# V in 1024-byte rows with its history copied on chip, head loads in other pieces, and a new written order

## The chip, the core and the metric

One core of a Trainium2 chip runs the whole program. It has a matrix engine (TensorE, PE in the profile; its weight loads are PEld), VectorE (DVE), ScalarE (ACT), GpSimd (POOL) and SyncE (SP), which here only issues DMA. Each engine works through its own list of instructions in order and waits on semaphores for the others. The metric is the device time of one launch in microseconds; the runs shown are compared by their median.

## What is computed

A block with adaptive layer norm: an attention over a dilated local window, then a gated FFN. S = 2048 rows, D = 512, 32 heads of 16, window of 8 keys at distance 2, FFN width 1792, all bf16.

```python
mod = (_silu(c) @ w_mod).reshape(c.shape[0], 6, 1, -1)
sa, ca, ga, sb, cb, gb = (mod[:, 0].copy(), ..., mod[:, 5].copy())
h = _layernorm(x, axis=-1) * (1 + ca) + sa
x = x + ga * _A_ref(h, A_wqkv, A_wo)
h = _layernorm(x, axis=-1) * (1 + cb) + sb
x = x + gb * _B_ref(h, B_w_gate, B_w_up, B_w_down)
...
# _A_ref: q, k, v from x @ wqkv; each query sees the keys at pos - 2*w, w = 0..7
logits = jnp.einsum('bhsd,bhswd->bhsw', q, kg) * scale
logits = jnp.where(mask[None, None, :, :], logits, -1000000000.0)
attn = _softmax(logits, axis=-1)
o = jnp.einsum('bhsw,bhswd->bhsd', attn, vg)
...
# _B_ref
h = _gelu(g) * u
return jnp.einsum('bsf,fd->bsd', h, w_down)
```

## The kernel before

The 2048 rows run as four groups (sg 0 to 3) of 512. For each group:

- `norm`, `norm_act`, `rst`, `norm_x`: statistics of x on DVE (`bn_stats`, `bn_aggr`, the "pair"), for some row blocks on ACT; a power on POOL gives 1/std; DVE writes the normalised `xn`, one instruction for each of four row blocks.
- xn is turned into hT (columns on partitions) and scaled by the modulation. There are three ways: for group 0 by PE transposes (`transp0`) with evictions on DVE and ACT (`transp0_ev`); for group 1's first norm and group 0's second (`BY_PE`) by PE transposes with evictions on ACT; for all others by a DMA transpose from SP (`transp`, L490), after which POOL (group 2's first norm, `H_POOL`) or ACT multiplies in place (`transp_ev`, L525 and L527).
- `qkv`: twelve blocks of four 512-column matmuls, the query, key and value rows with heads spread over partitions; ACT evicts them (`qkv_ev`). For group 0 the first two query blocks are made in halves of 256 columns (`qkv_halves`).
- `logits`: four DVE products `pq` of q with eight shifted views of kT (4096 elements per partition each), summed over the head's elements by PE matmuls with 32 output rows (`logits_mm`, the tile LTp). `soft`: max, subtraction, sum, reciprocal and product on DVE, the exponential on ACT; its result is `e`.
- `e` is spread to `PT`, for group 0 by PE and ACT (L736, L745), for the others through DRAM (`pt_dma`).
- V goes through DRAM: `vload` stores `vT` to `vscr` and reads it back four times (w4 = 0 to 3) into 32 partitions each of `V4`, each shifted by two rows more. Group sg reads 512 + 8 columns, the 8 being history from the group before; the zeros ahead of group 0 are written by POOL memsets.
- `pv`: four DVE products of PT and V4, summed by PE matmuls with 32 output rows (`pv_mm`, o_ps); `pv_ev` evicts to oT on ACT; `x1_mm` multiplies by wo, whose tile `woP` DVE has scaled by the gate `gB` (`woscale`); `x1_ev` adds to x.
- `ffn_mm`: 14 pairs of g and u (four matmuls each), gelu and eviction on ACT, product `hht` on DVE, then y by 56 matmuls and the addition `ot` on DVE, and the store.

The gates reach `gB` through DRAM (`gload`: a store of 1 KB and a broadcast read). Twenty warm-up matmuls (`warmup`) keep PE busy from the start until data is there; the first 11 run ahead of the transposition of silu(c).

Every step is an `Op` in one of 135 generators ("threads"), with an engine and the names it must come after. The list `ORDER` names, for the whole program, which thread gives its next step; this fixes the order on every engine, including the order in which SP issues its DMAs. Hardware DMAs share eight completion semaphores in rotation, so a DMA also waits until the one eight places ahead of it has landed.

SP's DMAs go out in this order at first: x of group 0 (half), the modulation columns 1 and 0 (`ldwm01`), wqkv0, x1, wqkv1, x2, wqkv2, the modulation columns 2 and 3, x3, four wo.

Of the kernel before, what the change touches and what calls it, by code (L numbers as in the profile page):

```python
# [106 lines left out]
def kernel(  # L107
# [23 lines left out]
    VH = 16  # L131
    VR = S + VH

# [5 lines left out]
    NB = {"x": 4, "hT": 2, "xn": 2, "q": 4, "vs": 1, "v4": 1, "prod": 5, "h2": 2,  # L139
# [17 lines left out]
    maskT = const.tile([H, W, 16], F32, name="maskT")  # L157
# [12 lines left out]
    kT = const.tile([P, 4, 3 * SG + 16], BF16, name="kT")  # L170

# [9 lines left out]
    def setup():  # L181
# [27 lines left out]
        yield Op("POOL", 3.0, f2, take=[SL["v4"]], fire="M2", after=["LN1.0.rs2"])  # L209
# [11 lines left out]
    def loads():  # L221
# [51 lines left out]
        def act_q():  # L273
            yield Op("ACT", 0.46, ldx(0, 2, 4, nc.scalar), fire="x0.2", lat=mb(0.25), dma=True)
            yield Op("ACT", 0.45, ldc, fire="c", lat=0.0, dma=True)
        qs = [act_q()]
        def head_q():
            yield Op("SP", 0.47, ldx(0, 0, 2), fire="x0.0", lat=mb(0.25))
            for b in (1, 0):
                yield Op("SP", 0.5, lambda b=b: ldwm01(b), take=[SL["prod"]] if b else [], fire=f"wm{b}", lat=mb(0.5))  # L280
# [697 lines left out]
```

## Time and profile before

| | us |
|---|---|
| median of 3 runs | 236.9 |
| lowest, highest | 236.7, 237.16 |
| span of the profiled execution | 234.1 |

How to read the profile: it shows one execution. Busy time is given per engine; matmuls are pipelined, so a single one's duration (379 ns for 512 columns) is longer than the distance from one to the next. The chain of waits goes back from the last instruction: at each step to what released it, or to the instruction ahead of it on its engine. A row of a timeline has start, duration, engine, source line, operation, output <- inputs, shapes, the number of instructions merged in it, and in brackets how long the engine stood idle before it and what ended that. "SPq" rows are DMA issues. In the tables by window the pairs are busy us and number of instructions for PE, PEld, DVE, ACT and POOL, then the granted clock, the DMA engines' share and GB/s.

The program reads 22.37 MB from HBM and writes 4.98 MB; SP's DMA queue keeps 16 DMA engines busy for 50.6% of the span, with 36265 packets in all, 14872 of them under 512 bytes.

### The profile page before, as it was taken

What the parts mean: (1) busy time and instruction counts of PE and PEld (TensorE: products, weight loads), DVE (VectorE), ACT (ScalarE), POOL (GpSimd) and SP (SyncE); (2) the same over time, 40 slices, a digit from 0 to 9 for tenths busy, and PEclk for the clock granted to TensorE, in tenths of its full rate; (3) what the DMA queues carried; (4) which work ended last, traced back from release to release, by engine and by line L of the source; (5) the groups of instructions that cost most, each with busy time, mean ns of one, the idle gap of its engine ahead of it and who ended that gap; (6) DMA issues with size and microseconds to landing.
All of it is one profiled execution on the core that took longest, in us unless ns stands there. A gap on an engine that the chain in (4) does not pass through costs nothing.

```text
span 234.1 us, 3675 instructions
## 1 busy us (share of the span) xinstructions
PE 230.0 (98%) x1387; PEld 108.2 (46%) x1387; DVE 170.4 (73%) x240; ACT 150.0 (64%) x283; POOL 18.6 (8%) x43
## 2 busy tenths in 40 slices
PE   7999999999999999999999999999999999999995
PEld 2755455434644444444444444444444444444443
DVE  3999999999997999999799788467747421222222
ACT  4899997976997758936656492546754343666400
POOL 2612461000100000100000010000001000000000
PEclk9999999999999999999999999999999999999999
DMA  6997989999969839553102963510000411000011
GB/s 218 373 364 213 202 213 171 276 391 303 176 152 236 291 92 200 98 114 103 56 0 57 202 109 60 156 56 0 0 4 0 90 45 45 3 0 0 0 48 45
DMA packets 36265, 30.21 MB, mean 129 GB/s; under 512 B 14872, under 2 KB 34328, under 8 KB 36248
## 3 DMA queue, kind: packets, MB, share of 16 engines
q1 hardware_dynamic: 35968, 29.72, 50.6%
q10 hardware_dynamic: 280, 0.26, 0.3%
q8 instruction: 11, 0.18, 0.3%
q14 instruction: 6, 0.05, 0.1%
HBM read 22.37 MB, written 4.98 MB: 117 GB/s over the span
## 4 chain that ended last, share of the span: by engine, by line
PE 98%; DVE 0%; issue 0%
PE g_ps L844 21%; PE u_ps L844 21%; PE y_ps L856 19%; PE qkv_ps L598 17%; PE x_ps L811 6%; PE o_ps L790 3%; PE LTp L678 3%; PE warm_ps L217 3%; PE y_ps L868 1%; PE qkv_ps L580 1%; PE hTp L484 1%; PE hTp L509 0%; PE modT_ps L305 0%; PE modT_ps L348 0%; PE gR_ps L369 0%; PE PTp L736 0%
## 5 line engine op out<-in xcount | busy, mean ns | idle before, releaser
L844 PE MATMUL g_ps<-h,Wg 128*128 128x512 bf16 x224 | 57.5, 379 | 0.0
L844 PE MATMUL u_ps<-h,Wu 128*128 128x512 bf16 x224 | 57.5, 379 | 0.0
L878 ACT ACTIVATE gl<-g_ps 128x512 bf16<-128x512 f32 x56 | 33.6, 600 | 24.8 <-PE g_ps L844 23.9
L856 PE MATMUL y_ps<-Wd,hht 128*128 128x512 bf16 x210 | 46.0, 379 | 0.0
L885 ACT CAST ub<-u_ps 128x512 bf16<-128x512 f32 x56 | 32.8, 586 | 18.3 <-PE u_ps L844 18.1
L598 PE MATMUL qkv_ps<-hT,wqkv 128*128 128x512 bf16 x184 | 42.1, 380 | 0.0
L896 DVE TENSOR_TENSOR hht<-gl,ub 128x512 bf16<-128x512 bf16 x56 | 23.0, 421 | 25.3 <-ACT ub L885 25.0
L664 DVE TENSOR_TENSOR pq<-qT,kT 128x4096 bf16<-128x4096 bf16 x16 | 36.3, 2292 | 0.0
L771 DVE TENSOR_TENSOR pv<-PT,V 128x4096 bf16<-128x4096 bf16 x16 | 36.0, 2286 | 0.0
L844 PEld LDWEIGHTS <-Wg 128*128 128x128 bf16 x224 | 21.5, 98 | 27.3 <-issue 2.1
L844 PEld LDWEIGHTS <-Wu 128*128 128x128 bf16 x224 | 21.8, 98 | 26.6 <-issue 0.4
L856 PEld LDWEIGHTS <-hht 128*128 128x128 bf16 x210 | 20.5, 98 | 24.8
L598 PEld LDWEIGHTS <-wqkv 128*128 128x128 bf16 x184 | 20.1, 114 | 19.7 <-issue 3.0
L903 DVE TENSOR_TENSOR ot<-y_ps,x 128x512 bf16<-128x512 f32 x15 | 10.3, 689 | 20.2 <-PE y_ps L856 17.2
L471 POOL TENSOR_TENSOR rstd<-rstd,neghalf 128x4 f32<-128x4 f32 (+1 forms) x9 | 8.8, 980 | 154.1 <-DVE rstd L460 85.5
L527 ACT ACTIVATE h<-h,modT,scl 128x512 bf16<-128x512 bf16 x12 | 8.8, 802 | 11.6 <-DMA h<-xn 11.6
L811 PE MATMUL x_ps<-woP,oT 128*128 128x512 bf16 x64 | 15.3, 379 | 0.0
L430 DVE BATCH_NORM_STATS2 st<-x 128x6 f32<-128x512 bf16 x19 | 12.9, 680 | 3.1 <-DMA x<-in_A_x_dram 2.9
L820 DVE TENSOR_TENSOR x<-x_ps,x 128x512 bf16<-128x512 f32 x16 | 10.8, 686 | 5.0 <-PE x_ps L811 5.0
L801 ACT CAST oT<-o_ps 128x512 bf16<-128x512 f32 x16 | 8.9, 592 | 2.7 <-PE o_ps L790 2.7
L618 ACT CAST qT<-qkv_ps 128x512 bf16<-128x512 f32 x16 | 9.2, 587 | 2.2 <-PE qkv_ps L598 2.1
L620 ACT CAST kT<-qkv_ps 128x512 bf16<-128x512 f32 x16 | 9.5, 596 | 1.2 <-PE qkv_ps L598 1.2
(85 smaller groups left out, 181.5 us busy)
## 6 DMA issues: line engine op xcount, KB each, us to landing
V<-vscr SPq DMA_DIRECT2D x12, 520.0 KB, 10.4
wm<-in_w_mod_dram SPq DMA_DIRECT2D x6, 512.0 KB, 5.4
vscr<-vT SPq DMA_DIRECT2D x4, 512.0 KB, 4.2
out_dram<-ot SPq DMA_DIRECT2D x15, 128.0 KB, 1.7
Wg<-in_B_w_gate_dram SPq DMA_DIRECT2D x1, 1792.0 KB, 11.0
Wu<-in_B_w_up_dram SPq DMA_DIRECT2D x1, 1792.0 KB
wqkv<-in_A_wqkv_dram SPq DMA_DIRECT2D x3, 512.0 KB, 8.3
x<-in_A_x_dram SPq DMA_DIRECT2D x3, 512.0 KB, 8.6
```

The lines of the kernel that those rows point to most:

```text
L430: nc.vector.bn_stats(out=st[:], in_=src()[:, c4, :])
L598: nc.tensor.matmul(ps[:], lhsT=wqkv[blk][:, dt, j::4], rhs=B["hT", sg][:, :, dt, :], start=(dt == 0), stop=(dt == DT - 1))
L664: nc.vector.tensor_tensor(out=pq[:], in0=_ap(B["qT", sg][:, j, :], [[0, W], [1, SG]]), in1=_ap(kT[:, j, sg % 3 * SG + 2:sg % 3 * SG + 2 + ...
L771: nc.vector.tensor_tensor(out=t[:], in0=_ap(B["PT", sg][:, 0, :], [[SG, 2], [0, 4], [1, SG]]), in1=_ap(v[:, 0, j, :], [[8, 2], [4 * (SG + ...
L811: nc.tensor.matmul(ps[:], lhsT=B["oT", sg][:, j, c4::CPS] if sg else B["oT", sg][:, j, c4 * P:(c4 + 1) * P], rhs=woP[:, j, :], start=(j == ...
L820: nc.vector.tensor_tensor(out=x[:, c4, :], in0=B["x1ps", sg, c4][:], in1=x[:, c4, :], op=ALU.add)
L844: nc.tensor.matmul(ps[:], lhsT=Wt[:, dt, ft * P:(ft + 1) * P], rhs=B["h2T", sg][:, :, dt, :], start=(dt == 0), stop=(dt == DT - 1))
L856: nc.tensor.matmul(ps[:], lhsT=B["hh", sg, ft][:, c4 * P:(c4 + 1) * P], rhs=B["Wd", ft // 4][:, ft % 4, :], start=(ft == 0), stop=(ft == F ...
L878: nc.scalar.activation(out=gl[:], in_=B["g", sg, ft][:], func=ACT.Gelu_apprx_tanh)
L885: nc.scalar.copy(out=ub[:], in_=B["u", sg, ft][:])
L896: nc.vector.tensor_tensor(out=hh[:], in0=B["gl", sg, ft][:], in1=B["ub", sg, ft][:], op=ALU.mult)
L903: nc.vector.tensor_tensor(out=ot[:], in0=B["y", sg, c4][:], in1=B["x", sg][:, c4, :], op=ALU.add)
```

## The change

- V: rows in `vscr` start at 64 elements instead of 16, each read is exactly 512 elements (1024 bytes) into columns 16 on of one fixed tile `V4`; the eight columns of history are copied within `V4` by POOL (`vhist`) once the group before has used them; the zeros ahead of group 0 come from one POOL memset and from 16 zero columns stored to `vscr` (`vzero`). The reads are a thread of their own (`vread`).
- Head: the modulation columns 0 and 1 are loaded as four pieces of 128 rows x 1024 columns (2048-byte rows) instead of two column blocks, and PE adds up their product piece by piece; wqkv0 is loaded in two halves; c is loaded from GpSimd's DMA queue instead of ACT's.
- Group 0: PE transposes one row block at a time; DVE and ACT share the evictions in another split (`ONV` for `PART`); three query blocks instead of two are made in halves; two warm-ups fewer. The mask tile becomes bf16.
- `ORDER` is another list. On SP, x1 now goes out ahead of the modulation pieces; wqkv0's halves, x2, wqkv1, wqkv2, modulation 2 and 3, the zero columns, x3 and modulation 4 follow. Among other moves: two `bn_stats` pairs of x1 stand on DVE ahead of group 0's last xn and its hT; group 2's first xn stand on DVE behind all four pq of group 0, and group 3's behind group 0's e and the second pq of group 1; the store of the first gate and the read of gB stand on SP behind group 3's DMA transpose, modulation 5 and two wo; three of V's four reads for group 1 stand behind the store of group 1's e; for group 1's second norm the first `ot` stands on DVE ahead of the four xn; in group 2 a pv stands between its second and third xn; group 3's second norm feeds g after 42 of group 2's y matmuls, the rest of which comes later.

```diff
-    VH = 16
+    VH = 64
     VR = S + VH
+    VW = SG + 16
...
-    maskT = const.tile([H, W, 16], F32, name="maskT")
+    maskT = const.tile([H, W, 16], BF16, name="maskT")
...
+    V4 = const.tile([P, 4, 4, VW], BF16, name="V4")
...
-            B["V4", 0] = T("v4", [P, 4, 4, SG + 8], BF16, "V4")
-            for w4 in range(4):
-                nc.gpsimd.memset(B["V4", 0][H * w4:H * w4 + H, :, :, 0:8 + 2 * w4].rearrange("p i j s -> p (i j) s"), 0.0)
+            nc.gpsimd.memset(V4[:, :, :, 0:16].rearrange("p i j s -> p (i j) s"), 0.0)
...
-        def ldwm01(b):
-            if "wm01" not in B:
-                B["wm01"] = T("prod", [P, 2, 4, D], BF16, "wm01")
-            nc.sync.dma_start(out=B["wm01"][:, b, :, :], in_=w_mod[:, b * D:(b + 1) * D].rearrange("(t p) n -> p t n", p=P))
+        def ldwm01(kt):
+            if kt == 0:
+                B["wm01"] = T("prod", [P, 4, 2 * D], BF16, "wm01")
+            nc.sync.dma_start(out=B["wm01"][:, kt, :], in_=w_mod[kt * P:(kt + 1) * P, 0:2 * D])
 
         def ldc():
-            nc.scalar.dma_start(out=c4[:], in_=c.rearrange("o (t p) -> (o t) p", p=P))
+            nc.gpsimd.dma_start(out=c4[:], in_=c.rearrange("o (t p) -> (o t) p", p=P))
...
+            for a in range(2):
+                yield Op("SP", 0.5, ld(wqkv[0][:, 2 * a:2 * a + 2, :], wq_v[:, 2 * a:2 * a + 2, 0:D]), fire=f"wqkv0.{a}", lat=mb(0.25))
...
+                for ch in range(8):
+                    nc.tensor.matmul(B["mp01"][:, ch:ch + 1], lhsT=B["wm01"][:, kt, ch * P:(ch + 1) * P],
+                                     rhs=scT[:, kt:kt + 1], start=(kt == 0 and ch == 0), stop=(kt == 3 and ch == 7))
...
-    PART = ((0, (0, 1), False), (0, (2, 3), True), (1, (0,), False), (1, (1, 2, 3), True))
+    ONV = {(0, True): (0, 2), (0, False): (1, 3), (1, True): (0, 1, 2), (1, False): (3,)}
...
+        for dt in range(DT):
+            def f(dt=dt):
+                for j in range(3):
+                    if dt == 0:
+                        B["qkvps", 0, 0, j] = T("mm", [P, SG], F32, "qkv_ps")
+                    mm(0, j, dt, dt)
...
+        for j in range(3):
+            def f(j=j):
+                for dt in range(DT):
+                    mm(1, j, dt, dt)
...
+    def vzero():
+        yield Op("SP", 0.6, lambda: nc.sync.dma_start(out=vscr[:, :, VH - 16:VH], in_=kT[:, :, 0:16]), after=["M2"],
+                 fire="vz", lat=1.2)
+
     def vload(sg):
         def f():
             nc.sync.dma_start(out=vscr[:, :, VH + sg * SG:VH + (sg + 1) * SG], in_=B["vT", sg][:])
...
+    def vhist(sg):
+        if sg:
+            def f():
+                nc.gpsimd.tensor_copy(out=V4[:, :, :, 8:16].rearrange("p i j s -> p (i j) s"),
+                                      in_=V4[:, :, :, VW - 8:VW].rearrange("p i j s -> p (i j) s"))
+            yield Op("POOL", 0.5, f, after=[f"pv.{sg - 1}.3"], fire=f"vh.{sg}")
+
+    def vread(sg):
         for w4 in range(4):
             def f(w4=w4):
-                if w4 == 0 and sg:
-                    B["V4", sg] = T("v4", [P, 4, 4, SG + 8], BF16, "V4")
-                z = 0 if sg else 8 + 2 * w4
-                src = bass.AP(vscr.tensor, vscr.offset + VH + sg * SG - 8 - 2 * w4 + z,
-                              [[16 * VR, H], [VR, 16], [1, SG + 8 - z]])
...
+                src = bass.AP(vscr.tensor, vscr.offset + VH + sg * SG - 2 * w4, [[16 * VR, H], [VR, 16], [1, SG]])
+                nc.sync.dma_start(out=V4[H * w4:H * w4 + H, :, :, 16:VW].rearrange("p i j s -> p (i j) s"), in_=src)
...
-                                        in1=_ap(v[:, 0, j, :], [[8, 2], [4 * (SG + 8), 4], [1, SG]]), op=ALU.mult)
...
+                                        in1=_ap(V4[:, 0, j, 8:16], [[8, 2], [4 * VW, 4], [1, SG]]), op=ALU.mult)
...
-    pl.spawn(warmup(13, 20))
+    pl.spawn(warmup(13, 18))
```

More of the change, by code (lines that the diff above doesn't have):

```diff
@@ L205, in f2 @@
                                         base=-H * w4, channel_multiplier=1)
[L206 to L209 removed]
+            nc.gpsimd.memset(V4[:, :, :, 0:16].rearrange("p i j s -> p (i j) s"), 0.0)
+        yield Op("POOL", 2.2, f2, fire="M2", after=["LN1.0.rs2"])
     def warmup(cold, n):
@@ L274, in act_q, with pool_q @@
             yield Op("ACT", 0.46, ldx(0, 2, 4, nc.scalar), fire="x0.2", lat=mb(0.25), dma=True)
-            yield Op("ACT", 0.45, ldc, fire="c", lat=0.0, dma=True)
-        qs = [act_q()]
+        def pool_q():
+            yield Op("POOL", 1.0, ldc, fire="c", lat=0.3, dma=True)
+        qs = [act_q(), pool_q()]
         def head_q():
             yield Op("SP", 0.47, ldx(0, 0, 2), fire="x0.0", lat=mb(0.25))
-            for b in (1, 0):
-                yield Op("SP", 0.5, lambda b=b: ldwm01(b), take=[SL["prod"]] if b else [], fire=f"wm{b}", lat=mb(0.5))
+            for kt in range(4):
+                yield Op("SP", 0.5, lambda kt=kt: ldwm01(kt), take=[] if kt else [SL["prod"]], fire=f"wm01.{kt}", lat=0.635)
+            for a in range(2):
+                yield Op("SP", 0.5, ld(wqkv[0][:, 2 * a:2 * a + 2, :], wq_v[:, 2 * a:2 * a + 2, 0:D]), fire=f"wqkv0.{a}", lat=mb(0.25))
         qs.append(head_q())
-        for b in range(3):
+        for b in range(1, 3):
             qs.append(one("SP", 0.55, ldq(b), fire=f"wqkv{b}", lat=mb(0.5)))
@@ L545, in f @@
                         nc.scalar.activation(out=o, in_=i, func=ACT.Identity, scale=sc(dt), bias=bi(dt))
-                yield Op("DVE" if onv else "ACT", 0.32 if onv else 0.455, f, after=[f"{ev}.th{half}"] + dep,
-                         take=[SL["hT"]] if dt == 0 and half == 0 else [], give=[SL["mm" if half else "att"]] if n == len(dts) - 1 else [],
-                         fire=f"{ev}.h{dt}.{half}")
+                give = [] if dt != ONV[half, eng][-1] else [SL["att"]] if half == 0 else [SL["lg" if eng else "mm"]]
+                yield Op("DVE" if eng else "ACT", 0.32 if eng else 0.455, f, after=[f"{ev}.th{2 * half + 1}"] + dep,
+                         take=[SL["hT"]] if dt == 0 and half == 0 else [], give=give, fire=f"{ev}.h{dt}.{half}")
     stat = pool("stat_p", 4)
@@ L570, with mm @@
     QKV = [(0, 0), (1, 0), (2, 0), (2, 1), (2, 2), (2, 3), (0, 1), (1, 1), (0, 2), (1, 2), (0, 3), (1, 3)]
-    QKV0 = [(0, 0), (0, 1), (0, 2), (1, 0), (1, 1), (0, 3), (1, 2), (2, 0), (2, 1), (2, 2), (2, 3), (1, 3)]
+    QKV0 = [(0, 0), (0, 1), (0, 2), (0, 3), (1, 0), (1, 1), (1, 2), (2, 0), (2, 1), (2, 2), (2, 3), (1, 3)]
     def qkv_halves():
-        for half in range(2):
-            for n, dt in enumerate(((2, 0, 3, 1), (0, 1, 2, 3))[half]):
-                def f(half=half, n=n, dt=dt):
-                    for j in range(2):
-                        if half == 0 and n == 0:
-                            B["qkvps", 0, 0, j] = T("mm", [P, SG], F32, "qkv_ps")
-                        nc.tensor.matmul(B["qkvps", 0, 0, j][:, half * 256:half * 256 + 256],
-                                         lhsT=wqkv[0][:, dt, j::4], rhs=B["hT", 0][:, 2 * half:2 * half + 2, dt, :],
-                                         start=(n == 0), stop=(n == DT - 1))
-                yield Op("PE", 0.218, f, after=[f"LN1.0.h{dt}.{half}", "wqkv0"],
-                         take=[SL["mm"]] * 2 + [SL["q"]] if half == 0 and n == 0 else [], fire=f"qph.{half}.{dt}")
-        for j in range(2):
-            pl.done[f"qp.0.0.{j}"] = pl.done["qph.1.3"]
+        def mm(half, j, dt, n):
+            nc.tensor.matmul(B["qkvps", 0, 0, j][:, half * 256:half * 256 + 256], lhsT=wqkv[0][:, dt, j::4],
+                             rhs=B["hT", 0][:, 2 * half:2 * half + 2, dt, :], start=(n == 0), stop=(n == DT - 1))
+        for dt in range(DT):
[4 more added lines that the diff above has]
+                    mm(0, j, dt, dt)
+            yield Op("PE", 0.328, f, after=[f"LN1.0.h{dt}.0", f"wqkv0.{dt // 2}"],
+                     take=[SL["mm"]] * 3 + [SL["q"]] if dt == 0 else [], fire=f"qph.{dt}")
+        for j in range(3):
+            def f(j=j):
+                for dt in range(DT):
+                    mm(1, j, dt, dt)
+            yield Op("PE", 0.437, f, after=[f"LN1.0.h{dt}.1" for dt in range(DT)], fire=f"qp.0.0.{j}")
     def qkv(sg):
@@ L591, in qkv @@
         for n, (blk, j) in enumerate(QKV if sg else QKV0):
[L592 removed]
+            if (sg, blk) == (0, 0) and j < 3:
                 continue
@@ L601, in qkv @@
             tk = {0: [SL["q"]], 1: [], 2: [SL["vs"]]}[blk] if j == 0 else []
-            yield Op("PE", 0.856, f, after=[f"LN1.{sg}.h{d}" for d in (("0.1", "1.0", "3.1") if sg == 0 else (2, 3))] + [f"wqkv{blk}"], take=[SL["mm"]] + tk,
+            yield Op("PE", 0.856, f, after=[f"LN1.{sg}.h{d}" for d in (("2.1", "3.1") if sg == 0 else (2, 3))] + ([f"wqkv{blk}"] if blk else []), take=[SL["mm"]] + tk,
                      give=[SL["hT"]] if last else [], fire=f"qp.{sg}.{blk}.{j}")
@@ L769, in f @@
                 B["pv", sg, j] = t
-                v = B["V4", sg]
                 nc.vector.tensor_tensor(out=t[:], in0=_ap(B["PT", sg][:, 0, :], [[SG, 2], [0, 4], [1, SG]]),
-                                        in1=_ap(v[:, 0, j, :], [[8, 2], [4 * (SG + 8), 4], [1, SG]]), op=ALU.mult)
-            yield Op("DVE", 2.2, f, after=[f"pt.{sg}.1", f"V4ld.{sg}"], take=[SL["prod"]] * heads(GV[sg]).get(j, 0),
-                     give=[SL["v4"], SL["PT"]] if j == 3 else [], fire=f"pv.{sg}.{j}")
+                                        in1=_ap(V4[:, 0, j, 8:16], [[8, 2], [4 * VW, 4], [1, SG]]), op=ALU.mult)
+            yield Op("DVE", 2.2, f, after=[f"pt.{sg}.1"] + [f"V4.{sg}.{w}" for w in range(3)] + [f"V4ld.{sg}"]
+                     + ([f"vh.{sg}"] if sg else ["M2"]), take=[SL["prod"]] * heads(GV[sg]).get(j, 0),
+                     give=[SL["PT"]] if j == 3 else [], fire=f"pv.{sg}.{j}")
     def pv_mm(sg):
```

73 lines of the change are left out of this document (34 added, 39 removed), and 70 rows, old and new, of the table ORDER.

## The prediction

> **What bounds it now.** The page first: the span, the busy shares, and the shares of the chain that ended last.
>
> ```profile
> span 234.1 us, 3675 instructions
> PE 230.0 (98%) x1387; PEld 108.2 (46%) x1387; DVE 170.4 (73%) x240; ACT 150.0 (64%) x283; POOL 18.6 (8%) x43
> ...
> PE 98%; DVE 0%; issue 0%
> ```
>
> TensorE (PE) is never without work: the chain is one row of matmuls. Nothing that only makes DMA lighter can pay. Three things can move the end: the time before the first useful matmul, the sum of the matmuls, and gaps that the new order opens. The chain in order of time (start, duration, what) gives the first two, and I read it next.
>
> ```profile
> 1.25 4.88 PE warm_ps L217 x11
> ...
> 10.07 1.85 PE qkv_ps L580 x16
> 11.93 7.77 PE qkv_ps L598 x36
> 19.70 0.45 PE hTp L484 x8
> ...
> 21.79 0.49 PE modT_ps L305 x16
> 22.28 0.55 PE LTp L678 x8
> ...
> 29.56 10.48 PE qkv_ps L598 x48
> ...
> 80.00 0.22 PE gR_ps L369 x16
> 80.23 0.43 PE o_ps L790 x8
> 80.66 0.97 PE g_ps L844 x4
> 81.63 0.86 PE u_ps L844 x4
> ...
> 97.64 12.09 PE y_ps L856 x56
> ```
>
> Useful work starts at 10.07. Four matmuls of 512 columns cost 0.86. Eight matmuls with 32-row outputs cost 0.43 inside a group of such, 0.55 as the first of one, and the four 512-column ones after the group 0.97 in place of 0.86: each group of 32-row work costs 0.12 + 0.11 = 0.23 of switching.
>
> **The sum of the matmuls.** After the head, PE's built order has 15 such groups before and 10 after: the matmuls of logits, of o and of the gates' rows are gathered. The counts are equal, but for eight more of 256 columns and four fewer of 512, which is even. Gain: 5 x 0.23 = **1.15 us**, all ahead of group 1's FFN (the 2048 rows run as groups 0 to 3).
>
> **The head.** Timeline of DVE and ACT (start, duration, what, idle before in brackets):
>
> ```profile
> 4.12 0.69 DVE L430 BATCH_NORM_STATS2 st<-x 128x6 f32<-128x512 bf16 x1 [2.94 <-DMA x<-in_A_x_dram]
> 4.60 0.31 ACT L328 ACTIVATE s<-c 4x128 bf16<-4x128 bf16 x1 [1.32 <-DMA c<-in_c_dram]
> 4.95 0.66 DVE L430 BATCH_NORM_STATS2 st<-x 128x6 f32<-128x512 bf16 x1
> 8.01 0.41 DVE L448 TENSOR_SCALAR xn<-x,mv,rstd 128x512 bf16<-128x512 bf16 x1 [0.27 <-POOL rstd L471]
> 8.34 0.41 DVE L448 TENSOR_SCALAR xn<-x,sums,rstd 128x512 bf16<-128x512 bf16 x1
> 8.98 1.68 DVE L543 TENSOR_SCALAR hT<-hTp,mod 128x256 bf16<-128x256 bf16 x5
> ```
>
> DVE works from 4.12 to 10.66 with hardly a pause but 0.27 us, so it, not the modulation rows, sets when hT is there. The new order puts two statistics pairs of x1 ahead of hT, 0.83 each (4.12 to 4.95). They fill the pause; and mod now stands before the last xn, which covers part of its latency, as the pairs cover that of the small operations: I take 0.4 for it, of the 8.98 - 8.34 - 0.41 = 0.23 seen there and as much again. So the last hT is done at 10.66 + 1.66 - 0.27 - 0.4 = 11.65 and the first (0.40 long, of five in 1.68) at 10.4; bounds 10.0 and 10.8. The 24 quarter matmuls at 1.85/16 = 0.116 end at 10.4 + 2.8 = 13.2, with three query blocks done; before, three were done at 11.93 + 0.86 = 12.8. Loss **0.4**. The two dropped warm-ups pay nothing, as PE waits for hT in their place.
>
> The head's loads, by windows (last column GB/s) and the tile view of wqkv:
>
> ```profile
> 5.00:10.00 5.00, 5.00 (x62) 2.98 (x61) 4.52 (x17) 4.09 (x11) 3.19 (x11) 1.00 1.07 365
> ...
> L223 SPq DMA_DIRECT2D wqkv<-in_A_wqkv_dram x3: 437/510/563, 2.4 to 5.0; - x3
> ...
> DMA to landing us min/median/max: 6.6/8.3/9.6
> ```
>
> wqkv0 stood behind 1.5 MB and landed at 2.4 + 6.6 = 9.0. After, x1's 0.5 MB goes ahead of the modulation rows, so their last piece takes that place, 9.0, and wqkv0's halves land 0.26 MB / 0.365 = 0.7 later each, at 9.7 and 10.4. The piece is wanted by 9.2 for a mod at 9.55, the halves at 10.4 and 11.1: covered, but by 0.2 at the tightest; what it is late beyond that the head loses. c landed at about 4.5 on ACT's queue. On GpSimd's it has no row; landing anywhere from 3 to 6 it moves only warm-ups, so no cost (rival C).
>
> **V.** PE waited for none of these:
>
> ```profile
> V<-vscr SPq DMA_DIRECT2D x12, 520.0 KB, 10.4
> vscr<-vT SPq DMA_DIRECT2D x4, 512.0 KB, 4.2
> ...
> PT<-escr SPq DMA_DIRECT2D x12, 64.0 KB, 2.4
> ...
> gB<-gscr SPq DMA_DIRECT2D x2, 128.0 KB, 2.8
> ```
>
> Lighter reads are therefore worth 0. The history copy waits on POOL for the last pv of the group before; behind it SP holds V's first part and, once, Wu, both wanted over 10 us later. Without that cover the copy would cost PE its own length, below 1 us.
>
> **New order, middle: hT of group 2.** It comes by a DMA transpose that SP issues, then by four multiplies on POOL.
>
> ```profile
> 20.88 8.89 DVE L664 TENSOR_TENSOR pq<-qT,kT 128x4096 bf16<-128x4096 bf16 x4
> 21.09 3.42 SPq L490 DMA_TRANSPOSE hT<-xn  x1
> 26.62 6.05 POOL L525 TENSOR_SCALAR hT<-hT,mod 128x512 bf16<-128x512 bf16 x4 [7.07 <-ACT gl L408]
> ...
> L525 POOL TENSOR_SCALAR hT<-hT,mod x4: 767/768/3802, 26.6 to 31.9; 128x512 bf16<-128x512 bf16 x4
> ...
> L527 ACT ACTIVATE hT<-hT,mod 128x512 bf16<-128x512 bf16 x4 | 3.0, 809 | 0.0
> ```
>
> Before, POOL is done at 32.67, and PE reads it ten blocks into the 29.56 row, at 38.2: 5.5 in reserve. After, DVE has from 11.65 on four statistics pairs, the small ones, twice four xn of 1.3 and four pq of 2.2 before xn of group 2 is whole: 11.65 + 3.3 + 0.4 + 2.6 + 8.8 = 26.75. SP is just then sending V's first read and one woP, since V's store had to land, so the transpose starts at 27.2. Its data is there 4.5 (99.75 to 104.23, below) to 5.5 (21.09 to 26.62) later, 31.7 to 32.7; four multiplies of 0.77 end at 34.8 to 35.8. PE wants it at 10.4 + 2.8 + 44 x 0.216 + 16 x 0.056 + 0.49 + (0.55 + 0.22 + 1.29) + 0.1 + 8.6 = 34.9: late by 0 to 0.9. POOL's row holds a worse case: its first multiply took 3.80 and ended 0.77 after 29.69, when the four pq of DVE's row had ended. After, a pq stands at about 35.1; a last multiply caught by it ends at 37.3, late by 2.4. The Trainium skill, "SBUF — State Buffer", section "SBUF: two separate sides", says that VectorE and GpSimd share a port pair by a lock, held for the whole instruction by whichever starts first. The 3.80 here agrees; by that rule the late case costs all of the 2.4, none shared.
>
> Next, hT of group 3: its xn end four pq and pv places on, at 38.7; data 43.2 to 44.2; ACT, which waits for it in order, then has four multiplies 0.7 apart and, with key and query evictions of 0.5 between, o's four: oT is whole at 50.0 to 50.5, where PE wants it at 49.4. And woP's scaling waits for gB, whose store now stands on SP behind this transpose (2 to 3.4 of SP), wm and two woP: sent by 43.6 at the latest, gB 1.6 or more later, landed in 2.8, at 47 to 49, scaled by 50.2. These three overlap in time: I take **0.9** for all, nearest to the oT row (bounds 0 and 2.5).
>
> **New order, FFN of group 1.** The rows of before:
>
> ```profile
> 98.64 1.05 DVE L448 TENSOR_SCALAR xn<-x,sums,rstd 128x512 bf16<-128x512 bf16 x3
> 99.75 2.02 SPq L490 DMA_TRANSPOSE h<-xn  x1
> 100.74 0.68 DVE L903 TENSOR_TENSOR ot<-y_ps,x 128x512 bf16<-128x512 f32 x1
> 104.23 2.93 ACT L527 ACTIVATE h<-h,modT,scl 128x512 bf16<-128x512 bf16 x4 [2.36 <-DMA h<-xn]
> ```
>
> Here all xn end ahead of the first ot, and h is whole at 107.16, 2.6 before PE's 97.64 + 12.09 = 109.73. After, the first ot, which waits for y's first quarter, stands ahead of all four xn. From y's start: 3.10 (97.64 to 100.74) + 0.62 + 1.4 + 4.48 + 2.93 + 0.05 = 12.55, while y lasts 12.09: PE waits 0.45, whatever came before. Group 2's chain, with one pv between its xn but no ot, comes out at 12.1 and just holds; group 3's, where only 42 y matmuls (9.06) cover it, at 9.2. Together **0.5** (bounds 0 and 0.9).
>
> **Sum.** 234.1 + 0.4 - 1.15 + 0.9 + 0.5 = 234.75 for the span. The median of the runs shown stands 2.8 above this span, and the difference is carried over: 236.9 + 0.65 = 237.55, said as 237.6.
>
> **Rivals.**
> A, the order holds, faster: gathering the 32-row groups (1.15) decides, if a transpose takes under 4 us from issue to first multiply; then the waits of the middle and the FFN are gone, and it is 236.9 + 0.4 - 1.15 = 236.15. For it: the order of before leaves not one wait on the chain, though much of it was as tight on DVE. Against: no transpose in the trace is that quick.
> B, the waits stack: POOL is caught by pq (2.4 in place of 0.9: 239.0), or V's last three parts for group 1 come late. They are now sent only after group 1's e, and reads of V moved 194 GB/s here:
>
> ```profile
> 58.00:60.00 2.00, 2.00 (x16) 1.06 (x15) 1.90 (x6) 2.00 (x5) 0.34 (x1) 1.00 1.13 194
> ```
>
> 1.57 MB then take 8.1, PT's loads 2.4 behind them and the sending 1, together 11.5, where four pq and two products leave 9.6; o has some 0.8 to spare, so 1.1 more: 238.7. Against both: the multiplies may start before the pq, and rows of exactly 1024 bytes leave no short piece.
> C, the clock: the eleven warm-ups took 0.44 each, against 0.216 later. If c comes late, scp stops PE between warm-ups, and full speed comes later; it costs half of what is still slow past 10.4. If 3.4 of the cold row's 4.88 fall there, 1.7 are lost: 239.3. The Trainium skill, "TensorE: Matmul & The Clock Gate", Part 1, has a free-running window of 3.4 us that must be busy; no run here shows its edge.
>
> **How the numbers follow.** 0.2% is about what a measurement can tell from no change: under 236.4 is faster, over 237.4 slower. The forecast has 0.40 (its own range 236.9 to 238.3; 0.13 of it within the bound, 0.27 slower), A 0.33 (0.29 faster, 0.04 within), B 0.17, C 0.10. So faster 0.29, same 0.17, slower 0.54. The range, 236.0 to 239.3, takes in A's value and B's two.
>
> **What would show it.** The first quarter matmul near 10.4; ten groups of 32-row work in the chain; a PE gap that ends on POOL near 35 or on ACT's oT near 50; and one of 0.4 before the g that follows the first 56 y. It is wrong if that last gap is missing, if the first quarter matmul starts before 10.0, or if PE's busy time, warm-ups apart, falls by less than 1 us.

## The result, and the profile after

| | us |
|---|---|
| before, median of 4 runs | 236.80 |
| changed, median of 4 runs (lowest, highest) | 250.74 (250.24, 251.41) |
| ratio, 95% interval | 1.0584, 1.0564 to 1.0605 |
| profiled execution of the changed kernel, its span | 250.51, 248.7 |

The change costs 13.9 us. Slower was forecast, but by 0.7 us, and the range ended at 239.3. First the page of the changed kernel:

```profile
span 248.7 us, 3677 instructions
PE 233.1 (94%) x1377; PEld 109.4 (44%) x1389; DVE 170.0 (68%) x240; ACT 149.4 (60%) x283; POOL 21.7 (9%) x44
...
PE 60%; DVE 15%; DMA 11%; issue 7%; ACT 3%; SPq 2%; POOL 1%; DVEq 0%; POOLq 0%
```

The chain was TensorE alone; now 40% of it lies on others. TensorE is idle more. Its waits (us in total, how many, the longest), and a table by stretch (from and to, us; then busy time and instructions of PE, PEld, DVE, ACT and POOL; granted clock; DMA share; GB/s):

```profile
PE o_ps L806 <- DVE pv L786: 2.9, 1, 2.9
PE qkv_ps L607 <- POOL hT L531: 2.7, 2, 2.5
...
PE g_ps L860 <- ACT h L533: 1.7, 4, 0.7
```

```profile
35.00:40.10 5.10, 2.24 (x8) 0.60 (x6) 3.65 (x4) 2.39 (x6) 5.10 (x5) 0.87 1.13 202
40.10:52.00 11.90, 11.87 (x65) 5.06 (x68) 8.08 (x7) 7.43 (x13) 0.95 (x1) 0.77 0.76 187
80.00:87.00 7.00, 4.08 (x32) 1.62 (x31) 3.53 (x3) 1.50 (x3) 0.00 (x0) 0.97 1.02 217
87.00:96.00 9.00, 9.00 (x68) 3.54 (x71) 8.47 (x9) 4.51 (x8) 0.70 (x1) 0.84 0.40 133
160.00:168.00 8.00, 6.22 (x27) 2.55 (x27) 8.00 (x6) 3.20 (x5) 0.00 (x0) 1.00 0.49 115
168.00:175.00 7.00, 6.14 (x52) 2.63 (x52) 2.27 (x6) 4.05 (x8) 0.00 (x0) 1.00 0.05 19
```

Idle time is the stretch less PE's busy time, and what the clock takes is estimated as the busy time by one less the clock. Around 40: 2.86 idle, and 0.13 x 2.24 + 0.23 x 11.87 = 3.0 by the clock. Around 85: 2.92, and 0.12 + 0.16 x 9.0 = 1.6. From 160 on: 1.78 + 0.86 = 2.6. Together 13.0, and the first useful matmul is 0.9 later. That is nearly all of the 14.6 by which the span grew. It says where the time is, not what would bring it back.

The first place, in a timeline of all engines:

```profile
13.30 1.03 POOL L472 TENSOR_TENSOR rstd<-rstd,neghalf 128x4 f32<-128x4 f32 x1 [1.60 <-DVE rstd L466]
...
23.55 2.28 DVE L680 TENSOR_TENSOR pq<-qT,kT 128x4096 bf16<-128x4096 bf16 x1
23.71 2.99 POOL L472 TENSOR_TENSOR rstd<-rstd,neghalf 128x4 f32<-128x4 f32 x1 [9.38 <-DVE rstd L466]
26.73 1.06 DVE L449 TENSOR_SCALAR xn<-x,mv,rstd 128x512 bf16<-128x512 bf16 x3 [0.91 <-POOL rstd L472]
...
28.48 3.03 SPq L491 DMA_TRANSPOSE hT<-xn  x1
...
34.92 5.16 POOL L531 TENSOR_SCALAR hT<-hT,mod 128x512 bf16<-128x512 bf16 x4 [8.22 <-ACT gl L420]
...
36.39 2.30 DVE L680 TENSOR_TENSOR pq<-qT,kT 128x4096 bf16<-128x4096 bf16 x1
...
39.38 0.59 PE L607 MATMUL qkv_ps<-hT,wqkv 128*128 128x512 bf16 x1 [2.51 <-POOL hT L531]
...
41.09 1.38 DVE L449 TENSOR_SCALAR xn<-x,sums,rstd 128x512 bf16<-128x512 bf16 x4 [2.40 <-POOL rstd L472]
```

Group 2's small power on GpSimd starts with the fourth pq and ends 0.87 us after it: 2.99 us for work that took 1.03 for group 1, at 13.30. xn is late by 0.9, the transpose is sent at 28.48, its data is multiplied from 34.92, and the multiplies last 5.16 for four of 0.77, as the next pq (36.39 to 38.69) falls among them. TensorE waits 2.51, and VectorE 2.40 for group 3's power, which stands behind those multiplies.

The second and third place, further on in the same view:

```profile
71.73 0.35 SPq L766 DMA_DIRECT2D escr<-e  x1
...
72.14 1.95 SPq L661 DMA_DIRECT2D V<-vscr  x3
...
74.19 2.64 SPq L774 DMA_DIRECT2D PT<-escr  x4
...
84.65 2.29 DVE L786 TENSOR_TENSOR pv<-PT,V 128x4096 bf16<-128x4096 bf16 x1 [3.47 <-DMA PT<-escr]
...
87.00 1.04 PE L806 MATMUL o_ps<-pv,Msum 128*32 128x512 bf16 x8 [2.92 <-DVE pv L786]
...
138.15 2.57 SPq L661 DMA_DIRECT2D V<-vscr  x4
...
145.92 0.33 SPq L766 DMA_DIRECT2D escr<-e  x1
...
152.49 2.54 SPq L774 DMA_DIRECT2D PT<-escr  x4
...
156.86 2.29 DVE L786 TENSOR_TENSOR pv<-PT,V 128x4096 bf16<-128x4096 bf16 x1 [2.71 <-DMA PT<-escr]
159.95 1.99 SPq L491 DMA_TRANSPOSE h<-xn  x1
```

Near 85, V's three parts for group 1 and PT's four are sent one behind the other, and the pv waits 3.47 for them on VectorE. The views of the tiles V and PT give the time from sending to landing, here of V's last read and of PT's last load:

```profile
L661 SPq DMA_DIRECT2D V<-vscr x1: 625/625/625, 73.5 to 73.5; - x1
...
DMA to landing us min/median/max: 9.3/9.3/9.3
...
L774 SPq DMA_DIRECT2D PT<-escr x1: 611/611/611, 76.2 to 76.2; - x1
...
DMA to landing us min/median/max: 8.2/8.2/8.2
```

V's last read landed at 82.8 and PT's last load at 84.4, just ahead of the pv at 84.65: the small loads came last, behind the reads. Near 160, e is stored behind four reads of V and takes 6.5 us where the store for group 1 took 2.1, so PT is late, and the pv that waits for it stands between the second and third xn of group 2's second norm: the transpose of h goes out at 159.95.

### The profile page after: what moved, and what is told of

Read it like the earlier page. It is cut to its first block, busy times and chain, and to the rows that moved or that the text cites. A ratio compares the mean times of both kernels' runs of the same rounds, so it can differ in the third digit from the quotient of the medians.

```text
span 248.7 us, 3677 instructions
## 1 busy us (share of the span) xinstructions
PE 233.1 (94%) x1377; PEld 109.4 (44%) x1389; DVE 170.0 (68%) x240; ACT 149.4 (60%) x283; POOL 21.7 (9%) x44
## 4 chain that ended last, share of the span: by engine, by line
PE 60%; DVE 15%; DMA 11%; issue 7%; ACT 3%; SPq 2%; POOL 1%; DVEq 0%; POOLq 0%
PE g_ps L860 13%; PE u_ps L860 13%; PE qkv_ps L607 12%; PE y_ps L872 10%; PE x_ps L827 4%; DVE pv L786 4%; DVE pq L680 3%; DMA escr<-e 3%; DMA hT<-xn 3%; PE o_ps L806 2%; DMA PT<-escr 2%; PE LTp L694 2%; DMA c<-in_c_dram 2%; DMA h<-xn 2%; SPq L774 1%
## 5 line engine op out<-in xcount | busy, mean ns | idle before, releaser
L860 PE MATMUL g_ps<-h,Wg 128*128 128x512 bf16 x224 | 58.9, 384 | 1.7 <-ACT h L533 1.7
L607 PE MATMUL qkv_ps<-hT,wqkv 128*128 128x512 bf16 x180 | 43.6, 395 | 3.3 <-POOL hT L531 2.7
L472 POOL TENSOR_TENSOR rstd<-rstd,neghalf 128x4 f32<-128x4 f32 (+1 forms) x9 | 10.6, 1174 | 95.9 <-DVE rstd L461 59.0
L806 PE MATMUL o_ps<-pv,Msum 128*32 128x512 bf16 x128 | 9.1, 395 | 3.7 <-DVE pv L786 2.9
L633 ACT CAST vT<-qkv_ps 128x512 bf16<-128x512 f32 x16 | 9.1, 598 | 2.3 <-PE qkv_ps L607 1.9
## 6 DMA issues: line engine op xcount, KB each, us to landing
Wg<-in_B_w_gate_dram SPq DMA_DIRECT2D x1, 1792.0 KB, 10.4
```

Source lines behind the costliest of these rows:

```text
L607: nc.tensor.matmul(ps[:], lhsT=wqkv[blk][:, dt, j::4], rhs=B["hT", sg][:, :, dt, :], start=(dt == 0), stop=(dt == DT - 1))
L806: nc.tensor.matmul(o_ps[H * i:H * i + H, :], lhsT=M2[:], rhs=B["pv", sg, j][:, t, i, :], start=(t == 0), stop=(t == 1), tile_position=(0, ...
L860: nc.tensor.matmul(ps[:], lhsT=Wt[:, dt, ft * P:(ft + 1) * P], rhs=B["h2T", sg][:, :, dt, :], start=(dt == 0), stop=(dt == DT - 1))
```

## Experiments

All times are medians; the kernel before took 236.70 to 236.81 in every set. In diffs of the order the list's thread numbers are written as steps: xn(g), pq(g,j), pv(g,j) for group g.

### Undoing one wait of the new order

The multiplies of hT of group 2 on ScalarE (p_scalar):

```diff
-    H_POOL = ('LN1.2',)
+    H_POOL = ()
```

> The changed kernel with one edit: the four multiplies that make hT of group 2 run on ScalarE instead of GpSimd; nothing is left out. Theory 1 (GpSimd's shared port with VectorE sets the middle gap: the fourth multiply lay from 36.98 to 39.31 behind a pq): ScalarE makes the four in about 2.9 us from 34.9, so TensorE waits 1 us instead of 2.7, too little for its clock to fall; 2.0 us of waiting and nearly all of the 2.7 us at half clock that followed go, and the time is about 246 us. Rival (the late transpose sets it, the multiplies add little): 249.5 or more. Rival (whatever is won is waited for again before the attention sum of group 1, where V is late): 249.5 or more, with the wait on pv grown from 2.9 to over 5 us.

250.92 us (249.83 to 252.79). Not what theory 1 said. The time is that of both rivals, but the wait on pv did not grow (2.9), and what the late transpose does by itself stays untested, since the multiplies did not come earlier: in the chain of waits the multiplies start only at 39.10, behind group 3's squares and group 1's evictions in ScalarE's order.

V's parts of group 1 early (v1_early):

```diff
 SP: ... V(1,0)  Wu
+    V(1,1) V(1,2) V(1,3)
     store of e(1)
-    V(1,1) V(1,2) V(1,3)
```

> The changed kernel with one edit: SyncE sends V's last three parts of group 1 right behind Wu, ahead of the store of group 1's weights (e), instead of behind it. Nothing is left out. Theory 1 (the order of sending makes pv of group 1 late): the 2.9 us that TensorE waits for pv near 85 and the 1.4 us at a lower clock behind it go: about 246.4 us. Rival (V's reads in the new layout are slow wherever they are sent): the wait stays over 1.5 us, 248.5 or more. Rival (they then slow Wu, which TensorE wants near 73): a new wait on Wu, 249 or more.

248.84 us, 1.9 less of the 4.3 expected, which is the time of the first rival. TensorE's wait for this pv is half as long (1.45 in place of 2.92). Now e's store is what the chain shows, behind the reads:

```profile
73.48 6.67 DMA escr<-e
```

c on ScalarE's queue (h_c_act):

```diff
-            nc.gpsimd.dma_start(out=c4[:], ...)
+            nc.scalar.dma_start(out=c4[:], ...)
```

> The changed kernel with one edit: c is loaded on ScalarE's queue again, as before, instead of GpSimd's. Theory 1: c lands near 4.5 instead of 5.9, the first quarter matmul starts at about 10.4 instead of 10.9, and the time falls by 0.5 us to about 250.2. Rival (the late c costs the clock of the head, as the prediction's case C had it): 1.5 to 2 us less, 249. Rival (the statistics on VectorE set the head alone): no change, 250.7.

249.79 us: 0.95 less, between the first and the second answer.

Idle stretches filled (d_dummies):

```diff
 PE: ... last k(1)
+    14 x matmul 128x512 (unused)
     q(2,0) ...
     logits(2) x16
+    12 x matmul 128x512 (unused)
     attention sum (1,0)
```

> The changed kernel with 14 matmuls of 512 columns added on TensorE ahead of group 2's queries and 12 ahead of the attention sum of group 1, each 0.216 us, which nothing uses: they fill the two gaps of 2.9 us or so and change no wait. Theory 1 (a third of the loss is the granted clock, which falls after a gap): the clock stays at 1.00 from 40 to 52 and from 87 to 96, and the 2.7 + 1.4 us lost there come back: about 246.6 us, although more work is done. Rival (the matmuls behind the gaps are slow for their own reasons, their operands come late): no gain, 250.7 or more.

250.62 us, with runs from 247.82 to 252.08. In the profiled run (251.39) the clock did what theory 1 said:

```profile
40.00:52.00 12.00, 11.55 (x84) 5.44 (x83) 9.20 (x9) 8.27 (x15) 2.50 (x3) 1.00 0.85 202
87.00:96.00 9.00, 8.62 (x75) 3.49 (x75) 9.00 (x10) 5.33 (x10) 0.70 (x1) 1.00 0.42 133
```

yet the median shows no gain, and pv's wait for its loads on VectorE was as long as before (3.6 us near 85, in the view of waits). This speaks for a second bound around 85, where VectorE waits for the loads whatever TensorE does. With runs 4.3 us apart and the lowest unprofiled, it is not shown.

The normalisation of group 2 early again (m_xn_early), then together with V's parts early and c on ScalarE's queue (mvh):

```diff
 DVE: ... stats(2)
+     rstd(2)
      xn(1) x4
+     xn(2) x4
      pq(0,0) pq(0,1) pq(0,2)
-     rstd(2)
      pq(0,3)
-     xn(2) x4
 SP:  ... wm2
+     transpose of xn(2)
      store of V(0)  V(0,0)  woP
-     transpose of xn(2)
```

> The changed kernel with one part of its order put back: the normalisation of group 2 (rstd, then its four xn) stands right behind group 1's on VectorE, ahead of the four pq of group 0, and SyncE sends its transpose ahead of V's store of group 0. Nothing is left out. Theory 2 (one late step, xn of group 2, holds both TensorE and VectorE, so that filling or shortening one gap alone gave nothing): the transpose starts near 23 instead of 28.5, hT of group 2 is whole by 34, TensorE does not wait for it, the rstd of group 3 no longer stands behind it on GpSimd, and everything from there on is 4 to 6 us earlier: 245 to 246.5 us. Rival (V's reads bound group 1, whatever comes before): the wait for pv near 85 grows by what was won, 249 or more.

> Three edits together: the normalisation and transpose of group 2 early (as in the run of it alone), V's last three parts of group 1 sent right behind Wu, and c on ScalarE's queue. Theory 2: 5 from the first, 2 to 3 from the second, 0.9 from the third, so 241.5 to 243 us; what is left over 236.8 belongs to groups 2 and 3, where all four parts of V are sent only after the last pv of the group before and the store of e stands behind them. Rival (one bound behind all of them): no better than 245.

255.54 us (252.28 to 256.45) and 247.60 us. The first is a clear miss, 9 us over; the second misses by 4.6, and its time is that of its rival (no better than 245). In the profiled run of the first (252.28) TensorE's wait for hT of group 2 is gone, but others came, 3.2 for pv and 3.1 for woP the longest. By VectorE's timeline group 2's statistics now wait 1.83 for ScalarE's squares, so that all pq come later, and woP waits 3.76 for the gate's rows. Mending single waits of the new order had brought 1.9 us at best, and all three together 3.1; so the parts were put into the old order instead.

### One part of the change alone, in the kernel before

V's rows, the copied history and the zeros (with the bf16 mask, which makes room), everything else as before:

```diff
 SP: ...
+    zeros to vscr
     store of V(0) ...
 POOL: ... 
+    copy history, ahead of group g's reads (g = 1, 2, 3)
```

> The kernel before, in its own order, with the V part of the change alone: rows of 1024 bytes, the history copied by GpSimd ahead of the reads, the zeros written to the scratch in DRAM; c and the head's loads as before. Theory 2 (the order costs, the layout is worth nothing): 236.3 to 237.3 us, reads of V still near 200 GB/s. Rival (the layout, the copy or the longer way of V's store costs by itself): 238.5 or more. Rival (lighter reads pay once the order doesn't spoil it): under 235.8.

236.63 us, ratio 0.999 (0.9981 to 0.9999). In the page's DMA part:

```profile
V<-vscr SPq DMA_DIRECT2D x16, 512.0 KB, 7.8
```

The 10.4 before is the median of the reads of groups 1 to 3; of all sixteen it is 8.7 (view of the tile V), against 7.8 now. Place for place little of that is left: the single read behind group 1's e lands in 5.5 before and 5.6 now, group 3's second and third in 7.6 and 9.4 before and 7.2 and 9.5 now, and only the reads of groups 1 and 2 gain some 2.4 and 1. Whether the rows made reads faster isn't shown. The whole part is worth about 0.2 us (0.02 to 0.45 by the interval), and TensorE has no wait for V in the kernel before.

c alone:

```diff
-            nc.scalar.dma_start(out=c4[:], ...)
+            nc.gpsimd.dma_start(out=c4[:], ...)
```

> The kernel before with one edit: c loaded on GpSimd's queue, ahead of GpSimd's constants, instead of ScalarE's. Theory: c lands 1.3 us later and the chain s, scp, scT and the modulation rows comes 0.5 to 0.9 later: 237.3 to 237.8 us. The prediction (it moves only warm-ups): 236.8. The prediction's case C (the clock of the head comes late): 238.5.

237.65 us: 0.84 more (ratio 1.002 to 1.0044), as expected. Its first useful matmul is 1.3 later (11.21 against 9.91 in the timelines).

### How much of the new order

The changed kernel, whole, with the new order up to a point and the order of before from there on:

```diff
 ORDER (by step)
-  new: all
+  b0:    head new, all else as before
+  a_mid: new up to pv(0,3)
+  a_g0:  new up to the last xn of group 0's second norm
+  a_y0:  new up to group 0's first y
+  a_x0:  new up to the second xn of group 2's second norm
```

> The changed kernel, whole (V, history copy, c on GpSimd's queue, the head's row pieces and halves), but behind the head every engine and queue issues in the order of before. Theory 3 (the order behind the head is the loss, by several waits, each behind another so that undoing one gives little): 236.8 and the 0.84 that c alone cost, so 237.2 to 238.2 us. Rival (the head's row pieces and halves cost as well): 239 or more. Rival (V's rows and copy cost when they meet this head): 239 or more, with waits for V.

> The changed kernel with the new order up to the last pv of group 0, and the order of before for all that is left. Theory 3 (three places; the middle with hT of group 2 is the largest): 5 to 6 over the kernel with the old order throughout, so 242 to 244.5 us. Rival (V's late reads for group 1 are the bound, the middle is covered): 240 or less. Rival (the later waits are echoes of the middle): 247 or more.

> The changed kernel with the new order up to the last xn of group 0's second norm, just ahead of its FFN, and the order of before for all that is left, V's second and third reads for group 1 ahead of e again among it. Theory 3: between the two others, 243 to 245 us. Rival (V late): 240 or less. Rival (echoes): as with the longer new order, 247 or more.

> The changed kernel with the new order up to the first y of group 0, and the order of before for all that is left, that is for the products of groups 2 and 3. Theory 3: only the place in group 2's second norm (3.3 us between the first y of group 1 and that of group 2) is gone: 246.5 to 248 us. Rival (it is an echo of the late start): 250 or more.

> The changed kernel with the new order up to the second xn of group 2's second norm, and the order of before for all that is left: pv of group 3 behind that norm's last xn and the attention sum of group 3 behind the eighth g of group 2. Theory 4 (the third place costs its 3.3 us between the first y of group 1 and that of group 2 by itself): 247 to 248.2 us. Rival (an echo, taken up elsewhere): 250 or more.

| new order up to | us |
|---|---|
| the head (b0) | 238.21 |
| pv(0,3) (a_mid) | 244.75 |
| ahead of group 0's FFN (a_g0) | 243.74 |
| group 0's first y (a_y0) | 251.02 |
| group 2's second norm (a_x0) | 247.38 |
| all of it | 250.74 |

The order behind the head is 12.5 of the 13.9 us. The middle is 6.5 of that by a_mid, a little over theory 3's 5 to 6, but a_mid has a wait of 1.34 (a logits group for its pq, at 56.59) at its own seam, where the new order passes into the old one; by a_g0 it is 5.5. a_y0 missed: there the waits of group 2's second norm are gone, but two new ones at the seam (y for hht 1.4, g for ot 0.7) and what follows them took their place. The later cut has no such seam and shows 3.4.

b0 took 1.5 more than the kernel before, and more than c's 0.84. Its head beside that of the changed kernel, TensorE's timelines, b0 first:

```profile
6.21 0.18 PE L336 MATMUL scp<-ident,s 4*128 4x4 bf16 x1 [1.79 <-ACT s L331]
6.32 2.74 PE L217 MATMUL warm_ps<-gB 128*128 128x512 bf16 x6
...
9.12 1.87 PE L217 MATMUL warm_ps<-gB 128*128 128x512 bf16 x4
...
12.93 1.25 PE L580 MATMUL qkv_ps<-hT,wqkv 128*128 128x256 bf16 x10
```

```profile
6.26 0.17 PE L336 MATMUL scp<-ident,s 4*128 4x4 bf16 x1 [1.85 <-ACT s L331]
6.37 1.47 PE L217 MATMUL warm_ps<-gB 128*128 128x512 bf16 x6
...
10.92 2.78 PE L580 MATMUL qkv_ps<-hT,wqkv 128*128 128x256 bf16 x24
```

The same wait for c, and then six warm-ups in 2.74 or in 1.47: in one execution TensorE goes on at half speed for 5 us, in the other it does not, and the first quarter matmul differs by 2.0. Of the ten profiled executions with this head and c on GpSimd's queue, seven show 2.74 for these six and three 1.47; the two with c on ScalarE's queue (h_c_act, mvh) show 1.47.

### One piece of the new order in the old one

Both in the kernel before with V's part (236.63):

```diff
 x1, DVE: xn(1) x4
-    rstd(2) xn(2) x4
     pq(0,1) pq(0,2)
+    rstd(2)
     pq(0,3)
+    xn(2) x4
 x1, SP: store of V(0)
-    transpose of xn(2)
     V(0,0)
+    transpose of xn(2)

 x2, SP: V(1,0)
-    V(1,1) V(1,2)
     store of e(1)
+    V(1,1) V(1,2)
     V(1,3)
```

> The kernel before with the V part of the change (236.63 us by itself) and one piece of the new order: group 2's rstd and four xn stand behind pq of group 0 (rstd behind the third, xn behind the fourth) and its transpose behind V's first read, as in the changed kernel. Theory 4 (this piece is the middle's cause: it delays hT of group 2, rstd of group 3 on GpSimd and V's reads together): 1.5 to 5 us more, 238 to 241.5 us, with a wait for hT on TensorE. Rival (the 5.5 us of reserve that hT has there hold it; the middle's loss needs the denser TensorE order as well): 237.3 or less, no wait for hT.

> The same kernel (old order with the V part, 236.63 us) and another single piece of the new order: V's second and third part for group 1 are sent behind e's store, as the fourth is in both. Theory 4 (V lands after it is wanted): the three parts are sent 14 us later, land near 78 where pv wants them at 75.7, and the time is 238 to 240 us. Rival (the reserve of 3 us and a quieter DMA hold it; V's lateness in the changed kernel came from the late e): 237.2 or less.

242.22 and 239.88 us: 5.59 and 3.25 more, each a cause by itself (x1 is 0.7 above the range expected). x1, TensorE's wait, then two rows of its chain and two stretches:

```profile
PE qkv_ps L598 <- POOL hT L525: 3.3, 4, 2.6
```

```profile
29.59 4.45 PE qkv_ps L598 x20
...
34.13 4.68 POOL hT L525 x4
```

```profile
34.00:40.00 6.00, 2.72 (x7) 0.86 (x7) 3.28 (x4) 1.27 (x3) 5.65 (x5) 0.76 1.00 250
40.00:45.00 5.00, 5.00 (x15) 1.89 (x14) 4.97 (x7) 1.77 (x5) 0.00 (x0) 0.60 1.19 184
```

3.3 of waiting and 0.24 x 2.72 + 0.40 x 5.0 = 2.65 by the clock: 5.95, of the 6.46 by which this execution (243.09) is longer; the median is 5.59 longer. x2, the chain:

```profile
71.48 7.90 DMA PT<-escr
...
79.40 4.50 DVE pv L773 x2
```

PT's last load needs 7.9 us behind V's reads; with V's part alone group 1's loads landed in 3.2 to 3.9. From V's first sending (67.09) to PT's landing (79.38) it is 12.3. TensorE waits 1.21 for the first pv and 1.28 for the second.

Then the waiting filled in x1, and both pieces together:

```diff
 x1d, PE: ...
+    11 x matmul 128x512 (unused)
     q(2,0) ...
 x12: the edits of x1 and of x2
```

> The kernel with group 2's normalisation late (242.22 us) and 11 matmuls of 0.216 us, which nothing uses, on TensorE ahead of group 2's first query block, where it waited 2.56 us for hT. Theory 4 (of the 5.6 us that this piece costs, the waits are 3.3 and the clock that falls to 0.60 behind them about 2.6): the clock stays at 1.00 and the time is 239.3 to 240 us, though TensorE does 2.4 us more. Rival (the slow matmuls behind the gap are not the gap's doing, or VectorE is the bound there): 242 or more.

> The old order with the V part and both pieces, group 2's normalisation late and V's three parts of group 1 behind e. Theory 4 (two causes, each with its own price): 242.22 + 3.25 = 245.5 us, within 0.8. Rival (the late start of everything covers V's lateness, or the two stack up): under 243.5, or over 247.

240.16 and 245.06 us. The same stretches of the first:

```profile
34.00:40.00 6.00, 4.89 (x22) 2.22 (x21) 4.04 (x5) 1.68 (x3) 5.31 (x5) 1.00 1.11 270
40.00:45.00 5.00, 5.00 (x44) 2.51 (x43) 4.97 (x6) 3.76 (x8) 0.00 (x0) 1.00 1.20 195
```

Doing 2.4 us of useless work makes the kernel 2.06 us faster (expected 2.2 to 2.9). In the old order, TensorE is the bound at that point, and the clock is worth most of the 2.65 that the rows say. And the two prices add up: 245.47 expected, 245.06 measured.

### Only what was to pay

The old order with V's part and two gatherings that ask nothing new of VectorE:

```diff
 PE: -logits(0,0)  q,k,v(1) x6  logits(0,1..3)
     +q,k,v(1) x6  logits(0,0..3)
     -sum(0,1)  k(2,3)  sum(0,2)
     +k(2,3)  sum(0,1)  sum(0,2)
```

> The old order with the V part and two gatherings of 32-row work on TensorE alone, none of them ahead of what VectorE has ready: group 0's first logits directly ahead of its others, and two attention sums of group 0 side by side. By 0.23 us each: 236.1 to 236.3 us, under both kernels. Rival (TensorE's switching isn't what the profile's rows said, or VectorE's order takes it back): 236.6 or more.

236.87 us, ratio 0.9997 to 1.002: no gain, with 13 groups of 32-row work in place of 15. No version tried lies below the kernel before by more than 0.2%.

## Why the prediction was wrong

| part | from | us |
|---|---|---|
| V's rows, history | V alone (236.63) against before | -0.2 |
| c on GpSimd | c alone (237.65) against before | +0.84 |
| the rest of the head | b0, less these two | +0.85 |
| xn of group 2 behind pq | x1 against V alone | +5.59 |
| V of group 1 behind e | x2 against V alone | +3.25 |
| group 2's second norm behind pv | changed against a_x0 | +3.36 |
| sum | | 13.7 |
| measured | | 13.94 |

The parts were measured in different surroundings, and that they add up was tried for the two largest alone.

**Head, forecast 0.4: mis-sized.** The profiled first quarter matmul came at 10.92, past the bound of 10.8. The step that failed is that c "moves only warm-ups", and so costs nothing. It landed at 5.9, inside the 3 to 6, but ScalarE takes silu(c) ahead of x's own sums and squares, so the row block that ScalarE normalises was late, and VectorE waited 0.29 for it and 0.18 for the modulation. The head as a whole costs 1.7 by the table, 0.84 of it by c alone; the rest is not taken apart by a run. Case C is one part of it, as it happens in some executions and not in others. The Trainium skill, "TensorE: Matmul & The Clock Gate", Part 1, has a free-running activity window, so that the number of slow matmuls differs between runs of one kernel. The two timelines above, of two kernels with one head, agree: 2.74 or 1.47 us behind an equal wait.

**Gathering, gain 1.15: not found.** Ten groups stand in TensorE's list, as said. But the prediction's own test fails. TensorE's busy time from the first quarter matmul to the end, in the old order (b0) and in the new one with the clock at 1.00 (mvh):

```profile
12.93:237.10 224.17, 221.28 (x1324) 104.41 (x1321) 163.99 (x220) 143.84 (x269) 17.53 (x14) 1.00 0.48 117
```

```profile
10.33:245.80 235.47, 222.70 (x1324) 104.83 (x1321) 163.35 (x220) 142.90 (x269) 14.55 (x19) 1.00 0.47 115
```

It did not fall by 1, it rose by 1.4. Part of that may be the new waits: a matmul behind one takes 0.38 to 0.59 on its own. What the switching is worth without them stays open; the kernel with two gatherings alone got nothing.

**V, 0: right.** It's about 0.2, and the cover of the history copy holds: TensorE waits for no copy.

**Middle, forecast 0.9, bounds 0 and 2.5: the step that failed most, 5.6.** The chain of causes was named rightly: late xn, late transpose, multiplies caught by a pq. Three things were wrong. First, the reserve in the kernel before, which made the move look safe, wasn't 5.5. x1, with TensorE's order of before, stops after 20 matmuls, five blocks and not ten into the row: at 34.0, while hT had been whole at 32.67. The reserve was 1.4. Second, the terms: xn was whole at 28.1 and not 26.75, because GpSimd's power was itself held by a pq; the transpose took 6.4 from sending to the first multiply and not 4.5 to 5.5; the caught multiply ended at 40.08 and not 37.3. TensorE came for it at 36.87 (39.38 less 2.51) and not 34.9, which hid 2 us of that; its waits for hT add up to 2.7. Third, the clock. The prediction priced it for the head alone, but behind a wait of 2.5 us it read 0.60 (x1) or 0.77 (the changed kernel) for 5 to 12 us; x1d, where it stays at 1.00, is 2.06 faster than x1. For group 0's oT and for woP, the other terms of the middle, TensorE did not wait.

The clock does not fall behind every such wait. In h_c_act TensorE waits 2.40 for the same hT, and in m_xn_early 3.21 for the pv near 90; the 12 us behind these:

```profile
39.59:51.59 12.00, 12.00 (x85) 5.73 (x84) 10.28 (x8) 9.71 (x18) 0.93 (x1) 1.00 0.83 199
```

```profile
90.27:102.27 12.00, 12.00 (x90) 5.21 (x90) 12.00 (x14) 6.81 (x13) 0.70 (x1) 1.00 0.52 139
```

The kept traces have seventeen waits of 2.3 to 3.2 us behind the head. In the 12 us behind them the clock reads 0.72 to 0.88 for thirteen and 1.00 for four.

The power took 2.99 us beside a pq, and ended 0.87 after it, against 1.03 (the row at 13.30) without. The Trainium skill, "SBUF — State Buffer", section "SBUF: two separate sides", has for the ports that VectorE and GpSimd share a lock that is held for the whole instruction; the trace agrees.

**V's last three parts, a rival at 1.1 us: right in kind, mis-sized.** It alone is 3.25. From V's sending to PT's landing the sum had 11.5, and x2 shows 12.3. The 1.1 it gave are near TensorE's wait for the first pv (1.21); it left out the second pv's (1.28). What makes up the rest of the 3.25 stays open.

**The FFN of group 1, 0.45: did not come.** The first ot stood 3.06 behind y's start, as forecast (3.10), and h was whole 12.37 behind it (forecast 12.55, though the terms add up to 12.58), but no wait precedes the g behind y: g starts at 120.69 and h is whole at 121.13, so g takes h's four parts one by one and need not have all of them.

**Group 2's second norm, "just holds": 3.4.** The sum counted the pv among its xn by its length. It is the wait in front of it that costs: V's four parts are sent after the last pv of the group before, e's store lies behind them (6.5 us), PT behind that.

**The cases.** They were set up as alternatives with a chance each, and the range reached to one at a time. They did not exclude each other, and nearly all happened at once: POOL caught by pq, V late, the clock, c. Only rival A, the order that holds, shuts out the rest.

## What to carry to other kernels

An order in which no engine waits has had its reserves spent on each other: when a step is moved, work out the reserve at its consumer by counting the instructions ahead of it, and price the wait in front of a moved instruction, not its length. A TensorE wait of some 2.5 us or more can cost half as much again, or as much again, by the clock, but need not (1.6 to 3.0 us behind the three worked out here, nothing behind four others or behind x2's two of 1.3): put that into the range, and put small loads ahead of large ones on a shared queue. Mishaps that don't exclude each other belong into one range together.

## What the runs showed of the hardware

- Behind a wait of 2.56 us and three matmuls in the next 2.2 us the granted clock read 0.60 for 5 us (x1); with 11 useless matmuls in its place it read 1.00, and 2.06 us were won. Behind waits of 2.40, 2.87, 3.13 and 3.21 us elsewhere (h_c_act, p_scalar, m_xn_early) it read 1.00 without any such filling.
- In the head the granted clock reads 1.00 in both executions shown, though warm-ups take 0.46 us each in the one and 0.25 in the other; there it is the durations that tell.
- A store of 256 KB took 6.5 us, and loads of 64 KB took 7.9 to 9.0, behind reads of 512 KB; by themselves 2.1, and 2.3 to 2.6.
